# A fused attention and maxout-FFN kernel: the scores of the stacked visits from scaled f16 halves, the last block's two heads in column tiles

## The chip, the cores and the metric

One of the cores of a Trainium2 chip runs the whole program. The metric is the device time of one execution in microseconds (us); lower is better. TensorE (PE) does matrix products, VectorE (DVE), ScalarE (ACT) and GpSimd (POOL) do elementwise work, SyncE (SP) issues the DMAs.

## The reference

Inputs are q, k, v (8 batches, 8 heads, 576 positions, 64 elements per head, f32), s (8, 8, 576) and the FFN's weights (w1, w2, w3: 512 x 768, w_out: 768 x 512, f64). Causal attention with a positional bias is followed by a maxout FFN over the 4608 tokens:

```
scores = q @ k.T / 8
cum    = cumsum(max(s, 0))
bias   = -(cum[:, None] - cum[None, :])
scores = where(key later than query, -1e9, scores + min(bias, 0))
attn   = softmax(scores)
x      = attn @ v                     # heads side by side: 4608 x 512
out    = max(x @ w1, x @ w2, x @ w3) @ w_out
```

Over the keys that count, the bias of one row is cum[key] minus a constant of the row, which the softmax cancels.

## The kernel before

**Visits and steps.** The kernel works on pairs of heads. A visit is one pair of one batch with some of its five query blocks (four of 128 rows and a last one of 64, `qb` 0 to 4); a step is one query block of one visit, and there are 160 of them in a list. The first two batches are visited twice (16 visits, 40 steps). Each of the other six batches has four visits of five steps; these 24 visits, 16 to 39, are the **stacked** ones (function `stacked`), and they make steps 40 to 159.

**Scores of a stacked visit.** [...] In `h`, 64 partitions hold the rounded half of q and 64 the rest of q, against the rounded half of k twice. In `l`, 64 partitions hold the rounded half of q against the rest of k, and 64 ("own") hold the bias: columns of ones that select rows of `kb`, a table of the cumulated s. So `scores` (L411) issues four matmuls for a query block: `h` and `l` for head j = 0 and 1, each with 128 weight columns and (qb + 1) x 128 key columns. The last block has only 64 rows a head: its two heads lie in the two halves of one 128-column weight that is zero-padded, so L422 issues eight matmuls (`h`, `l`, two heads, 256 and 320 keys), and L427 adds the causal mask of the last 64 keys by a matmul. `highest` takes the row's maximum: with a mask from SBUF in the custom DVE operation of L508 for blocks 0 to 3, and as a plain reduction (L513) for the last block.

**Making h and l.** `load_head` (L148) brings q and k of one head, twice over, to a raw tile. `head_qhi` and `head_khi` (ACT, L177, L181) round, `head_qlo` (DVE L186, POOL L190) and `head_klo` (POOL L195) form the rests and copies, `head_bias` (POOL, L164 to L170) writes the "own" half. The two heads of a visit are prepared over the five or so steps before its first step.

**What follows a step's scores.** `expo` (ACT), `probs` (DVE reciprocal L551, ACT L567, DVE L570: f16 high and low parts), DMA transposes from SP's queue, and `values` (PE, L698; two 64-column tiles side by side, one per head). Scores of two steps are in flight: `ps_s` has two buffers, so the scores of step t + 2 wait until L570 of step t has read its own.

**The FFN in between.** When all four pairs of a batch have their rows, `add_set` puts 18 groups of 12 matmuls (L830) and 4 of 18 (L872), all f16 with 128 weight columns and 256 or 320 moving ones, into `queue`. ACT and DVE (L844, L847) take the groups out of PSUM (three buffers), POOL splits the result (L836, L837).

**The order.** The main loop writes each step's work in a fixed order; `at(t, f, ...)` puts a function into step t, and the table `moved` shifts some. Up to step 59 a table `GROUPS` says how many FFN groups a step gets. After that a budget does: each step adds `STEP_NS` less the estimate `pe_cost` of its own PE work, and groups run while the budget is positive:

```
cost[0] = min(cost[0] + (4400.0 if t < 60 else STEP_NS) - pe_cost(t), 4000.0)
```

Behind the last step the remaining groups run alone. The tables of the bias are made at the start: `cumulate` (DVE) and `spread` (PE L278 to L284, ACT L289 to L294, POOL L295), once for pairs 0 to 15 and once for 16 to 31. `power` makes a power of two from a maximum (L309), for the values' and the weights' scales.

Of the kernel before, what the change touches and what calls it, by code (L numbers as in the profile page):

```python
# [21 lines left out]
def kernel(  # L22
# [5 lines left out]
    qk: bass.AP,  # L28
    s: bass.AP,
# [28 lines left out]
    STEP_NS = 4700.0  # L58
# [73 lines left out]
    def below(t):  # L132
        v, qb = steps[t]
        return stacked(v) and qb < 4
# [4 lines left out]
    def load_head(v, j):  # L139
        b, g, _ = visits[v]  # L140
        r = R.setdefault(v, {})
        if v == 2 * NP * NB:
            for n, (x, c0, c1) in enumerate((("rq", 0, QP), ("rk", QP, V0))):
# [4 lines left out]
        nc.sync.dma_start(out=t, in_=qk[b, g, j])  # L148
        r["rq", j], r["rk", j] = t[:, 0:QP], t[:, QP:V0]

    def head_bias(v, j):

        r = R.setdefault(v, {})
        if j == 0:
            h = att.tile([P, V0], F32R, tag="qkh", name=f"h{v}_0")
            l = att.tile([P, V0], F32R, tag="qkl", name=f"l{v}_0")
        else:
            h = wpool.tile([P, V0], F32R, tag=f"w{18 + v % 2}", name=f"h{v}_1")
            l = wpool.tile([P, V0], F32R, tag=f"w{20 + v % 2}", name=f"l{v}_1")
        r["h", j], r["l", j] = h, l  # L160
        pair = visits[v][0] * NP + visits[v][1]
        kb, qr, sl = KB[pair // 16], QR[pair // 16], pair % 16
        own = slice(j * D, (j + 1) * D)
        nc.gpsimd.tensor_copy(out=l[own, QP:V0], in_=kb[own].bitcast(F32))  # L164
        nc.gpsimd.tensor_copy(
            out=l[own, 0:Q4].rearrange("p (a c) -> p a c", c=P),
            in_=qr[own, sl, 0:4].bitcast(F32).unsqueeze(2).to_broadcast([D, 4, P]),
        )
        nc.gpsimd.memset(l[own, Q4 + (1 - j) * D:Q4 + (2 - j) * D].bitcast(F32), 0.0)
        nc.gpsimd.tensor_copy(  # L170
            out=l[own, Q4 + j * D:Q4 + (j + 1) * D], in_=qr[own, sl, 4:5].bitcast(F32).to_broadcast([D, D])
        )


    def head_qhi(v, j):
        raw, h = R[v]["rq", j], R[v]["h", j]
        nc.scalar.activation(out=h[:, 0:QP], in_=raw, func=AF.Copy, scale=SCALE)  # L177

    def head_khi(v, j):
        raw, h = R[v]["rk", j], R[v]["h", j]  # L180
        nc.scalar.activation(out=h[:, QP:V0], in_=raw, func=AF.Copy)  # L181

    def head_qlo(v, j):
# [3 lines left out]
            out=h[own, 0:QP], in0=raw[own], scalar=SCALE, in1=h[own, 0:QP].bitcast(F32),  # L187
            op0=ALU.mult, op1=ALU.subtract,
        )
        nc.gpsimd.tensor_copy(out=l[far, 0:QP], in_=h[far, 0:QP].bitcast(F32))  # L190

    def head_klo(v, j):
        raw, h, l = (R[v][x, j] for x in ("rk", "h", "l"))
        far = slice((1 - j) * D, (2 - j) * D)
        nc.gpsimd.tensor_tensor(  # L195
            out=l[far, QP:V0], in0=raw[far], in1=h[far, QP:V0].bitcast(F32), op=ALU.subtract
        )

# [41 lines left out]
    sel = io.tile([HB, 2, 2, 160], F32R, tag="raw", name="sel", bufs=2)  # L240
    nc.gpsimd.memset(sel.bitcast(F32), 0.0)
    for j in range(2):
        nc.gpsimd.memset(ones[64 * j + 32:64 * j + 64, 0:1], 1.0)
        nc.gpsimd.memset(ones[64 * j:64 * j + 32, 1:2], 1.0)
        for T in range(2):
# [56 lines left out]
    def power(am, name):  # L302

        amb = small.tile([P, 1], BF16, tag="amb", name=f"amb{name}")
        nc.vector.tensor_scalar(
            out=amb, in0=am, scalar1=2.0 ** -80, scalar2=2.0 ** 127, op0=ALU.max, op1=ALU.min
        )
        gm = ps_m.tile([P, 512], F32, tag="m", name=f"gm{name}")
        nc.tensor.matmul(gm[:, :P], lhsT=amb.to_broadcast([P, P]), rhs=identb, start=True, stop=True)  # L309
# [12 lines left out]
    def vscale1(k):  # L322
        am = small.tile([P, 1], F32, tag="am1", name=f"am1{k[0]}_{k[1]}")
        nc.vector.tensor_reduce(out=am, in_=AM.pop(k), axis=AX.X, op=ALU.max)
        VS[k] = power(am, f"v{k[0]}_{k[1]}")
# [26 lines left out]
    def prep3(v):  # L352
# [41 lines left out]
    def scores(t):  # L394
# [3 lines left out]
        pair = b * NP + g  # L398
        kb, qr, sl = KB[pair // 16], QR[pair // 16], pair % 16
        ps = ps_s.tile([P, 2, 512], F32, tag="s", name=f"s{t}")  # L400
        nm = small.tile([P, 2], F32, tag="nm", name=f"nm{t}")
        if stacked(v):
            flat = ps.rearrange("p a n -> p (a n)")
            n0 = min(qb * P, Q4)
            qs = slice(n0, n0 + P)
            nk = qs.stop
            for x in "hl":
                for j in range(2):
                    w = r[x, j]
                    if qb < 4:  # L410
                        nc.tensor.matmul(  # L411
                            ps[:, j, :nk], lhsT=w[:, qs], rhs=w[:, QP:QP + nk], start=(x == "h"), stop=(x == "l"),
# [14 lines left out]
            nc.tensor.matmul(  # L427
                flat[:, 768:832], lhsT=identb, rhs=tri4, start=False, stop=True, skip_group_check=True
            )
            U[t] = (flat[:, 256:832], nm[:, 0:1], S)  # L430
            return
        if v < NPS:
# [65 lines left out]
    def later_keys():  # L498
        m = wpool.tile([P, Q4], BF16, tag="w23", name="later")
        nc.gpsimd.memset(m[:, 0:Q4 - P], 0.0)  # L500
        nc.gpsimd.tensor_copy(out=m[:, Q4 - P:Q4], in_=tri)
        future.append(m)

    def highest(t):
        sc, nm, nk = U[t]
        if below(t):
            for j in range(2):
                nc.vector.tensor_tensor_reduce(  # L508
                    out=sc[:, j], in0=sc[:, j], in1=future[0][:, Q4 - nk:Q4], scale=-1.0, scalar=3.0e38,
# [470 lines left out]
    def amid(t, f, *a):  # L980
# [3 lines left out]
        {("head_klo", 18, 0): -1, ("head_klo", 19, 1): -1, ("head_qlo", 18, 1): -1, ("later_keys",): 1,  # L984
        ("load", 4): -2, ("load", 5): -3, ("load", 6): -4, ("load", 7): -5, ("load_head", 16, 0): -7,
# [255 lines left out]
```

## Time and profile before

| | us |
|---|---|
| runs of the kernel before: median of 3 (lowest to highest) | 873.72 (872.49 to 875.30) |
| the profiled execution's own time | 874.56 |
| its span, first to last instruction | 872.7 |
| busy in the span: PE / DVE / ACT / POOL | 830.6 / 578.2 / 565.3 / 330.5 |

The span is what the trace's rows add up to; the execution's own time lies 1.9 us above it, and the median of the runs 0.8 us below that own time. A chain row of the trace gives the PE's time from one piece's end to the next one's, so it is what a piece really takes of PE; the mean duration of a matmul row is longer, since matmuls overlap.

### The profile page before, as it was taken

What the parts mean: (1) busy time and instruction counts of PE and PEld (TensorE: products, weight loads), DVE (VectorE), ACT (ScalarE), POOL (GpSimd) and SP (SyncE); (2) the same over time, 40 slices, a digit from 0 to 9 for tenths busy, and PEclk for the clock granted to TensorE, in tenths of its full rate; (3) what the DMA queues carried; (4) which work ended last, traced back from release to release, by engine and by line L of the source; (5) the groups of instructions that cost most, each with busy time, mean ns of one, the idle gap of its engine ahead of it and who ended that gap; (6) DMA issues with size and microseconds to landing.
All of it is one profiled execution on the core that took longest, in us unless ns stands there. A gap on an engine that the chain in (4) does not pass through costs nothing.

```text
span 872.7 us, 19483 instructions
## 1 busy us (share of the span) xinstructions
PE 830.6 (95%) x6919; PEld 653.8 (75%) x6919; DVE 578.2 (66%) x1454; ACT 565.3 (65%) x1500; POOL 330.5 (38%) x534
## 2 busy tenths in 40 slices
PE   4988999999998899999999999999999999999998
PEld 3876778777776678777887788777877788778875
DVE  5989976777766667766767667666767666753110
ACT  5878786677766656767676666677766776754111
POOL 3001113325535245453545446455435545421211
PEclk9999999999999999999999999999999999999999
DMA  9933557878665665778665778669766786534000
GB/s 353 353 89 83 121 134 166 187 147 162 139 138 138 149 143 122 155 141 173 128 146 131 154 137 163 133 129 172 144 153 129 145 139 137 106 73 88 13 14 31
DMA packets 234449, 121.25 MB, mean 139 GB/s; under 512 B 209456, under 2 KB 218160, under 8 KB 234352
## 3 DMA queue, kind: packets, MB, share of 16 engines
q1 hardware_dynamic: 233776, 118.43, 61.9%
q10 hardware_dynamic: 576, 1.57, 0.5%
q8 instruction: 55, 0.90, 0.5%
q14 instruction: 42, 0.34, 0.2%
HBM read 60.70 MB, written 9.44 MB: 80 GB/s over the span
## 4 chain that ended last, share of the span: by engine, by line
PE 57%; DVE 3%; POOL 3%; ACT 2%; issue 1%; DMA 1%; POOLq 0%; DVEq 0%; ACTq 0%
PE pm L830 33%; PE po L872 12%; PE s L411 6%; PE av L698 5%; PE s L422 2%; DVE prl L570 1%; ACT prh L567 1%; POOL hh L836 1%; DVE m L847 1%; POOL l L195 1%; DMA ph<-prh 1%; ACT s L527 1%; POOL hl L837 0%; POOL l L164 0%; DVE s L508 0%
## 5 line engine op out<-in xcount | busy, mean ns | idle before, releaser
L830 PE MATMUL pm<-x,w 128*128 128x320 f16 (+1 forms) x3240 | 426.2, 288 | 1.3 <-DVE x L708 1.2
L830 PEld LDWEIGHTS <-w 128*128 128x128 f16 x3240 | 308.4, 98 | 88.2 <-issue 6.8
L567 ACT ACTIVATE prh<-s,ri 128x512 f16<-128x512 f32 (+3 forms) x272 | 136.2, 546 | 70.9 <-DVE ri L551 68.1
L570 DVE SCALAR_TENSOR_TENSOR prl<-s,ri,prh 128x512 f16<-128x512 f32 (+3 forms) x272 | 147.0, 577 | 44.2 <-ACT prh L567 26.1
L836 POOL CAST hh<-m 128x320 f16<-128x320 f32 (+1 forms) x90 | 51.3, 570 | 301.3 <-DVE m L847 217.7
L847 DVE SCALAR_TENSOR_TENSOR m<-pm,m 128x320 f32<-128x320 f32 (+1 forms) x180 | 82.2, 457 | 124.9 <-PE pm L830 102.4
L527 ACT ACTIVATE s<-s,nm 128x128 f32<-128x128 f32 (+4 forms) x272 | 144.9, 533 | 10.1 <-DVE nm L508 5.6
L872 PE MATMUL po<-hh,w 128*128 128x320 f16 (+1 forms) x720 | 140.9, 287 | 0.0
L872 PEld LDWEIGHTS <-w 128*128 128x128 f16 x1080 | 103.2, 98 | 31.9 <-issue 4.5
L508 DVE CUSTOM_DVE_ANT_0 s<-s,later 128x128 f32<-128x128 f32 (+1 forms) x192 | 94.5, 492 | 32.0 <-PE s L411 28.7
L872 PE MATMUL po<-hl,w 128*128 128x320 f16 (+1 forms) x360 | 103.2, 287 | 0.9 <-POOL hl L837 0.9
L844 ACT ACTIVATE m<-pm 128x320 f32<-128x320 f32 (+1 forms) x90 | 36.8, 409 | 91.1 <-PE pm L830 89.3
L837 POOL TENSOR_TENSOR hl<-m,hh 128x320 f16<-128x320 f32 (+1 forms) x90 | 70.7, 786 | 7.3
L195 POOL TENSOR_TENSOR l<-raw,h 64x576 fp32r<-64x576 f32 x46 | 64.4, 1401 | 8.7 <-ACT h L181 7.3
L880 ACT ACTIVATE o<-po,os 128x320 f32<-128x320 f32 (+1 forms) x60 | 30.0, 501 | 58.1 <-PE po L872 51.8
L164 POOL CAST l<-kb 64x576 fp32r<-64x576 f32 x48 | 32.2, 671 | 80.5 <-PE s L422 79.3
L513 DVE TENSOR_REDUCE nm<-s 128x1 f32<-128x576 f32 (+3 forms) x64 | 49.8, 778 | 17.6 <-PE s L427 10.7
L698 PEld LDWEIGHTS <-vh 128*64 128x64 f16 x800 | 43.5, 110 | 21.0 <-issue 15.7
L411 PE MATMUL s<-h 128*128 128x128 f32 (+1 forms) x192 | 54.0, 362 | 4.7 <-DVE prl L570 4.6
L527 ACT ACTIVATION_READ_ACCUMULATOR s<-s,nm 128x1 f32 x272 | 54.2, 199 | 0.0
L698 PE MATMUL av<-ph,vh 128*64 128x320 f16 (+3 forms) x368 | 48.0, 282 | 2.1 <-DMA ph<-prh 2.1
L707 ACT ACTIVATE x<-av 128x320 f16<-128x320 f32 (+1 forms) x60 | 24.7, 412 | 37.4 <-PE av L698 36.3
(161 smaller groups left out, 1167.7 us busy)
## 6 DMA issues: line engine op xcount, KB each, us to landing
raw<-in_qk_dram SPq DMA_DIRECT2D x46, 608.0 KB, 4.7
r<-in_w_dram SPq DMA_DIRECT2D x22, 512.0 KB, 8.4
rv<-in_qkv_dram SPq DMA_DIRECT2D x32, 320.0 KB, 3.1
out_dram<-o SPq DMA_DIRECT2D x32, 160.0 KB, 2.1
out_dram<-o SPq DMA_DIRECT2D x32, 128.0 KB, 1.9
raw<-in_qkv_dram SPq DMA_DIRECT2D x8, 480.0 KB, 4.0
ph<-prh SPq DMA_TRANSPOSE x184, 3.3
pl<-prl SPq DMA_TRANSPOSE x184, 2.8
```

Source lines behind the costliest of these rows:

```text
L195: nc.gpsimd.tensor_tensor(out=l[far, QP:V0], in0=raw[far], in1=h[far, QP:V0].bitcast(F32), op=ALU.subtract)
L411: nc.tensor.matmul(ps[:, j, :nk], lhsT=w[:, qs], rhs=w[:, QP:QP + nk], start=(x == "h"), stop=(x == "l"), skip_group_check=True,)
L508: nc.vector.tensor_tensor_reduce(out=sc[:, j], in0=sc[:, j], in1=future[0][:, Q4 - nk:Q4], scale=-1.0, scalar=3.0e38, op0=ALU.add, op1=ALU ...
L527: nc.scalar.activation(out=E[t][:, j, :nk] if plain else sc, in_=sc, func=AF.Exp, bias=nm[:, j:j + 1], scale=-1.0 if below(t) else 1.0, ac ...
L567: nc.scalar.activation(out=hi, in_=src, func=AF.Copy, scale=sc)
L570: nc.vector.scalar_tensor_tensor(out=lo, in0=src, scalar=sc, in1=hi, op0=ALU.mult, op1=ALU.subtract)
L698: nc.tensor.matmul(av[j * D:(j + 1) * D, c0:nq], lhsT=lt, rhs=rt, start=(n < 2), stop=(n >= len(todo) - 2), skip_group_check=True,)
L830: nc.tensor.matmul(pm[:, :nq], lhsT=w[:, wt, kt, :], rhs=xt, start=(n == 0), stop=(n == 3 * NKT - 1))
L836: nc.gpsimd.tensor_copy(out=st["hh"][:, ft, :nq], in_=m1[:, :nq])
L837: nc.gpsimd.tensor_tensor(out=st["hl"][:, ft, :nq], in0=m1[:, :nq], in1=st["hh"][:, ft, :nq], op=ALU.subtract)
L847: nc.vector.scalar_tensor_tensor(out=m1[:, :nq], in0=pm[:, :nq], scalar=HSC, in1=m1[:, :nq], op0=ALU.mult, op1=ALU.max)
L872: nc.tensor.matmul(pm[:, :nq], lhsT=W[18 + ft][:, wt, dt, :], rhs=st[ht][:, ft, :nq], start=(n == 0), stop=(n == 3 * NFT - 1),)
```

## The change

Only the stacked visits change in their arithmetic; their four products per head pair are the same four.

- `h` and `l` become f16. For that, q and k of each batch are scaled by powers of two: `load_pair` (SP) brings q and k of a pair once more in another layout (128 partitions x 1152, 576 KB), `pair_max` (two DVE reductions over 576 columns) takes their largest magnitudes, and `pair_scale1` to `pair_scale3` make the batch's scales (DVE, two PE matmuls, eight small POOL operations). This runs 10 to 30 steps ahead of the batch.
- The bias of the last six batches no longer comes from `spread(1)` at the start. s is loaded again at step 22, cumulated, and cut into three f16 pieces (`bias1` to `bias3`, steps 23 to 25, POOL and DVE), and `bias4` spreads them at steps 27 to 29 with nine f16 matmuls each.
- The last block's two heads are no longer padded: L566 writes head j with 64 weight columns to partitions 64 j on, so that its eight matmuls are four pairs in two column tiles. The mask matmul goes; `highest` uses the custom DVE operation with a mask there too (L652).
- Per head, POOL loses a memset, copies the key half of the bias only for 2 visits of 8, and gets one more operation: the rest of k needs k multiplied by its scale first (new L195, in place), then the subtraction (new L198). q and its columns shrink from 640 to 576.
- `STEP_NS` goes from 4700 to 4520, `pe_cost` gets a new estimate for stacked steps, and `moved` gets many entries, so the FFN groups fall on the steps in another way.

The diff, cut to its core:

```diff
-    STEP_NS = 4700.0
+    STEP_NS = 4520.0
...
     def below(t):
         v, qb = steps[t]
-        return stacked(v) and qb < 4
+        return stacked(v)
...
     def head_bias(v, j):
...
+            h = att.tile([P, 2 * S], F16, tag="qkh", name=f"h{v}_0")
...
-        nc.gpsimd.tensor_copy(out=l[own, QP:V0], in_=kb[own].bitcast(F32))
+        if (v - 2 * NP * NB) % (2 * NP) < 2:
+            nc.gpsimd.tensor_copy(out=l[own, S:2 * S], in_=kb[own])
...
     def head_klo(v, j):
...
+        nc.gpsimd.tensor_scalar(
+            out=raw[far], in0=raw[far], scalar1=QK[visits[v][0]]["k"][far], scalar2=None, op0=ALU.mult
+        )
+        nc.gpsimd.tensor_tensor(out=l[far, S:2 * S], in0=raw[far], in1=h[far, S:2 * S], op=ALU.subtract)
...
+    def bias4(G):
...
+        for i in range(3):
+            nc.tensor.matmul(ka, lhsT=sl[:, i, 32:160], rhs=pc[:, i, 0:512], start=(i == 0), stop=(i == 2))
+        for i in range(3):
+            nc.tensor.matmul(kc[:, 0:64], lhsT=sl[:, i, 32:160], rhs=pc[:, i, 512:S], start=(i == 0), stop=(i == 2))
+        for i in range(3):
+            nc.tensor.matmul(
+                kc[:, 64:69], lhsT=sl[:, i, 0:128], rhs=cn[:, i], start=False, stop=(i == 2), skip_group_check=True
+            )
...
+    def load_pair(v):
+        b, g, _ = visits[v]
+        ST[v] = wpool.tile([P, V0], F32, tag=f"w{tag_of(v)}", name=f"pair{v}")[:, 0:2 * S]
+        nc.sync.dma_start(out=ST[v], in_=pair[b - NB, g])
...
+    def pair_max(v, x):
...
+        nc.vector.tensor_reduce(
+            out=QK[b]["m"][:, x, g:g + 1], in_=ST[v][:, x * S:(x + 1) * S], axis=AX.X, op=ALU.max,
+            apply_absolute_value=True,
+        )
...
                         nc.tensor.matmul(
-                            flat[:, o:o + nk], lhsT=w[:, qs], rhs=w[:, QP + k0:QP + k0 + nk],
-                            start=(x == "h" and j == 0), stop=(x == "l" and j == 1 and k0 == 0),
-                            skip_group_check=True,
+                            flat[j * D:(j + 1) * D, o:o + nk], lhsT=w[:, Q4:S], rhs=w[:, S + k0:S + k0 + nk],
+                            start=(x == "h"), stop=(x == "l"), skip_group_check=True,
                         )
-            nc.tensor.matmul(
-                flat[:, 768:832], lhsT=identb, rhs=tri4, start=False, stop=True, skip_group_check=True
-            )
...
             nk = min((steps[t + 2][1] + 1) * P, S)
-            c += max(4 * nk * NSEC * 1.09, 480.0) + (100.0 if nk < S else 150.0)
+            if stacked(steps[t + 2][0]):
+                c += 2 * S * NSEC + 250.0 if nk == S else 4 * nk * NSEC + 40.0
+            else:
+                c += max(4 * nk * NSEC * 1.09, 480.0) + (100.0 if nk < S else 150.0)
...
-            at(first[w] + (4 if w % NP == 0 else 2), vmax, v)
+            at(first[w] + (4 if w % NP == 0 else VM if stacked(w) else 2), vmax, v)
...
+        o = (21, 24, 27, 27)[g] if b == NB else first[v - g] - 30 + PM[3] + 5 * g
+        at(o, load_pair, v)
+        for x in range(2):
+            at(o + (2 if b == NB else PM[x]), pair_max, v, x)
...
-    spread(1)
```

**POOL, between visit 24 and visit 25** (`raw25_1` is the second head of visit 25, `l26_0` or `l16_0` the first operand of visit 26; `hh`, `hl` are the FFN's). Before:

```order
L164 CAST l26_0_6164<-kb1_226 64x576
L165 CAST l26_0_6164<-qr1_229 64x512
L169 MEMSET l26_0_6164 64x64
L170 CAST l26_0_6164<-qr1_229 64x64
L195 TENSOR_TENSOR l25_1_5983<-raw25_1_5826,h25_1_5982 64x576
L190 CAST l26_0_6164<-h26_0_6163 64x640
```

With the change:

```order
L190 COPY x17_1_3195<-x17_1_3195 64x576
L195 TENSOR_SCALAR raw25_1_6026<-raw25_1_6026,qf4_5447 64x576
L198 TENSOR_TENSOR x17_1_3195<-raw25_1_6026,x17_1_3195 64x576
L985 CAST hh3_0_6087<-m13_0_3_6330 128x256
L986 TENSOR_TENSOR hl3_0_6088<-m13_0_3_6330,hh3_0_6087 128x256
L170 COPY l16_0_2745<-qr164_5455 64x512
L173 COPY l16_0_2745<-qr164_5455 64x64
```

The second head's rest of k stood behind the next visit's bias columns; now it stands ahead of them, with the new multiplication before it.

**DVE, at the turn from visit 25 to visit 26** (right behind `probs` of visit 25's last block; `m1` are FFN groups; `prl90` belongs to the first block of visit 26, and its end frees the PSUM buffer for the scores of step 92; `am28` is `vmax` for a later visit's v). Before:

```order
L847 SCALAR_TENSOR_TENSOR m13_1_1_6683<-pm3_1_1_1_6656,m13_1_1_6683 128x320
L847 SCALAR_TENSOR_TENSOR m13_1_1_6683<-pm3_1_1_2_6686,m13_1_1_6683 128x320
L551 RECIPROCAL ri90_6732<-se90_6708 128x2
L508 ISA s91_6699,nm91_6700<-s91_6699,later_1562 128x256
L508 ISA nm91_6700 128x1
L508 ISA s91_6699,nm91_6700<-s91_6699,later_1562 128x256
L508 ISA nm91_6700 128x1
L570 SCALAR_TENSOR_TENSOR prl90_6735<-s90_6623,ri90_6732,prh90_6734 128x128 x2
```

With the change:

```order
L996 SCALAR_TENSOR_TENSOR m13_1_1_6851<-pm3_1_1_1_6856,m13_1_1_6851 128x320
L996 SCALAR_TENSOR_TENSOR m13_1_1_6851<-pm3_1_1_2_6884,m13_1_1_6851 128x320
L466 TENSOR_REDUCE am28_6528<-rv29_6632 128x1
L298 TENSOR_REDUCE qm5_5611<-pair31_6536 128x1
L305 TENSOR_REDUCE qa5_6918<-qm5_5611 128x2
L446 TENSOR_SCALAR ambq5_6920<-qa5_6918 128x2
L700 RECIPROCAL ri90_6952<-se90_6906 128x2
L657 ISA s91_6897,nm91_6898<-s91_6897,later_1543,qf4_5447 128x256
L657 ISA nm91_6898 128x1
L657 ISA s91_6897,nm91_6898<-s91_6897,later_1543,qf4_5447 128x256
L657 ISA nm91_6898 128x1
L719 SCALAR_TENSOR_TENSOR prl90_6955<-s90_6841,ri90_6952,prh90_6954 128x128 x2
```

`vmax` has come here from the visit's third step, and a `pair_max` (with, once a batch, the two small operations of `pair_scale1`) stands behind it, both ahead of the reciprocal that `prl90` needs. The other `pair_max` of each visit stands in the third step, where `vmax` was.

## Rows read from the trace of the kernel before

**Rows 1.** The page's part 1: span, then busy time and share of each engine.

```profile
span 872.7 us, 19483 instructions
PE 830.6 (95%) x6919; PEld 653.8 (75%) x6919; DVE 578.2 (66%) x1454; ACT 565.3 (65%) x1500; POOL 330.5 (38%) x534
```

**Rows 2.** Busy time by stretch: length, PE, PEld, DVE, ACT, POOL, PE clock, DMA share, GB/s.

```profile
213.00:798.00 585.00, 570.99 (x4896) 446.82 (x4895) 398.23 (x1077) 399.63 (x1073) 268.77 (x426) 0.99 0.68 139
798.00:872.70 74.70, 71.23 (x593) 56.39 (x590) 11.48 (x25) 9.36 (x21) 14.36 (x26) 1.00 0.07 22
```

**Rows 3.** PE's waits from 213 to 800 us: total us, times, longest.

```profile
PE s L411 <- DVE prl L570: 4.6, 7, 0.9
PE s L422 <- DVE prl L570: 3.3, 3, 2.7
PE av L698 <- DMA pl<-prl: 2.0, 1, 2.0
PE s L411 <- POOL l L195: 0.7, 2, 0.4
```

**Rows 4.** The chain that ended last, 540 to 600 us: start, us, what.

```profile
559.66 0.47 PE s L411 x4
...
563.41 0.70 PE s L411 x4
...
565.76 1.65 PE av L698 x28
567.41 1.74 PE pm L830 x12
569.15 0.92 PE s L411 x4
570.07 3.27 PE pm L830 x24
...
578.64 0.40 PE s L411 x4
...
598.43 1.06 PE s L422 x8
599.49 0.04 PE s L427
```

**Rows 5.** The same chain, 408 to 420 us.

```profile
413.53 3.94 PE pm L830 x36
...
418.19 0.07 PE gmv L309
```

**Rows 6.** PE's timeline at 187 us: start, us, engine, line, operation, shapes.

```profile
187.57 0.29 PE L471 MATMUL s<-tri,identb 128*128 128x128 bf16 x2
```

**Rows 7.** One matmul of that line by itself: duration ns, least/median/most.

```profile
L471 PE MATMUL s<-tri,identb x32: 219/224/230, 91.1 to 203.3; 128*128 128x128 bf16 x32
```

**Rows 8.** Groups by line and shape: busy us, mean ns of one, idle before.

```profile
L195 POOL TENSOR_TENSOR l<-raw,h 64x576 fp32r<-64x576 f32 x46 | 64.4, 1401 | 8.7 <-ACT h L181 7.3
...
L164 POOL CAST l<-kb 64x576 fp32r<-64x576 f32 x48 | 32.2, 671 | 80.5 <-PE s L422 79.3
...
L318 DVE TENSOR_REDUCE am<-rv 128x1 f32<-128x640 f32 x32 | 25.8, 810 | 1.3 <-DMA rv<-in_qkv_dram 1.3
```

**Rows 9.** DVE's and PE's timelines at one turn of visits.

```profile
561.21 0.60 DVE L570 SCALAR_TENSOR_TENSOR prl<-s,ri,prh 128x128 f16<-128x128 f32 x2
...
563.14 0.62 PE L411 MATMUL s<-h 128*128 128x384 f32 x2
```

**Rows 10.** The start: ACT's and PE's timelines.

```profile
14.04 0.69 ACT L289 ACTIVATE kb<-ka,ones 128x512 fp32r<-128x512 f32 x1 [1.34 <-PE ka L278]
...
15.05 0.65 ACT L732 ACTIVATE t<-r 128x512 f32<-128x512 f32 x1
...
18.18 0.79 PE L601 MATMUL pp<-dg,e 128*128 128x128 f32 x2 [3.52 <-ACT dg L595]
```

**Rows 11.** DMA issues: KB each, us to landing.

```profile
raw<-in_qk_dram SPq DMA_DIRECT2D x46, 608.0 KB, 4.7
```

More of the change, by code (lines that the diff above doesn't have):

```diff
@@ L28 @@
     qk: bass.AP,
+    pair: bass.AP,
     s: bass.AP,
@@ L186, in head_qlo @@
         nc.vector.scalar_tensor_tensor(
-            out=h[own, 0:QP], in0=raw[own], scalar=SCALE, in1=h[own, 0:QP].bitcast(F32),
+            out=h[own, 0:S], in0=raw[own], scalar=QK[visits[v][0]]["q"][own], in1=h[own, 0:S],
             op0=ALU.mult, op1=ALU.subtract,
         )
-        nc.gpsimd.tensor_copy(out=l[far, 0:QP], in_=h[far, 0:QP].bitcast(F32))
+        nc.gpsimd.tensor_copy(out=l[far, 0:S], in_=h[far, 0:S])
     def head_klo(v, j):
@@ new lines, in bias1 @@
+    def bias1():
+        nc.gpsimd.memset(BS["m"], 0.0)
+        nc.gpsimd.tensor_scalar(out=BS["s"], in0=BS["s"], scalar1=0.0, scalar2=None, op0=ALU.max)
+        t = wpool.tile([P, 2 * V0], F16, tag="w19", name="pieces")[0:HB]
+        BS.update(
+            pc=t[:, 0:3 * S].rearrange("p (i c) -> p i c", c=S),
+            cn=t[:, 3 * S:3 * S + 15].rearrange("p (i c) -> p i c", c=5),
+            sl=t[:, 3 * S + 16:3 * S + 496].rearrange("p (i c) -> p i c", c=160),
+        )
+        select(0)
@@ new lines, in pair_max, with pair_scale1 @@
+    def pair_max(v, x):
+        b, g, _ = visits[v]
+        if b not in QK:
+            QK[b] = dict(m=small.tile([P, 2, NP], F32, tag="qm", name=f"qm{b}", bufs=2))
+        nc.vector.tensor_reduce(
+            out=QK[b]["m"][:, x, g:g + 1], in_=ST[v][:, x * S:(x + 1) * S], axis=AX.X, op=ALU.max,
+            apply_absolute_value=True,
+        )
+    def pair_scale1(b):
+        am = small.tile([P, 2], F32, tag="qa", name=f"qa{b}", bufs=2)
+        nc.vector.tensor_reduce(out=am, in_=QK[b]["m"], axis=AX.X, op=ALU.max)
+        QK[b]["a"] = clamp(am, f"q{b}", 2)
@@ L244 @@
         nc.gpsimd.memset(ones[64 * j:64 * j + 32, 1:2], 1.0)
-        for T in range(2):
+        for T in range(1):
             a = 32 * j + 16 * T
@@ L307, in power @@
         )
+        return amb
+    def power(amb, name, n=1):
         gm = ps_m.tile([P, 512], F32, tag="m", name=f"gm{name}")
-        nc.tensor.matmul(gm[:, :P], lhsT=amb.to_broadcast([P, P]), rhs=identb, start=True, stop=True)
+        for i in range(n):
+            nc.tensor.matmul(
+                gm[:, i * P:(i + 1) * P], lhsT=amb[:, i:i + 1].to_broadcast([P, P]), rhs=identb, start=True, stop=True
+            )
         return gm
@@ L498, in later_keys @@
     def later_keys():
[L499 to L500 removed]
+        m = wpool.tile([P, Q4 + S], BF16, tag="w23", name="later")
+        nc.gpsimd.memset(m, 0.0)
         nc.gpsimd.tensor_copy(out=m[:, Q4 - P:Q4], in_=tri)
[L502 removed]
+        nc.gpsimd.tensor_copy(out=m[:, 2 * Q4:2 * Q4 + D], in_=tri4)
+        future.extend((m[:, 0:Q4], m[:, Q4:Q4 + S]))
     def highest(t):
@@ L1106 @@
     at(20, later_keys)
+    at(22, load_bias)
+    at(23, bias1)
+    at(24, bias2)
+    soon(25, bias_power)
+    at(25, bias3)
+    for n in range(3):
+        at(27 + n, bias4, n)
+    for v in range(2 * NP * NB, len(visits)):
+        b, g, _ = visits[v]
+        o = (21, 24, 27, 27)[g] if b == NB else first[v - g] - 30 + PM[3] + 5 * g
+        at(o, load_pair, v)
+        for x in range(2):
+            at(o + (2 if b == NB else PM[x]), pair_max, v, x)
+        if g == NP - 1:
+            e = o + (3 if b == NB else PM[2])
+            at(e - 1, pair_scale1, b)
+            soon(e, pair_scale2, b)
+            at(e, pair_scale3, b)
     prep2(0)
```

190 lines of the change are left out of this document (151 added, 39 removed).

## The prediction

> **What bounds the kernel now.** I read the busy times first, then the stretches, then who waits for whom, then the chain. PE is busy for 95% of the span and no other engine for more than 66% [rows 1]. The stacked steps lie between 213 and 798 us: there PE is idle for 585.0 - 571.0 = 14 us, while DVE and ACT are busy for 68% and POOL for 46%. Behind 798 us only FFN groups are left, and PE runs alone for 75 us [rows 2]. PE's waits in the stacked steps are few: about 8 us for DVE's `prl`, 2 for a transpose, 0.7 for POOL [rows 3]. The chain is mostly PE, piece after piece [rows 4]. So a microsecond of PE work taken out is a microsecond of time, as long as the other engines keep the pace; the clock share is 0.99 in the stacked steps, the upper of its two levels, and nothing here should change that. The groups that the new budget moves between steps cancel out: the same FFN matmuls run in all, and by the written order only 2.4 us more of them stand before the last step.
>
> **PE, the scores.** Chain rows give what a block costs now: 0.40 us for 128 keys, 0.47 for 256, 0.70 for 384, 0.92 for 512, and 1.06 + 0.04 = 1.10 for the last block with its mask [rows 4]. For f16 the FFN's matmuls give 3.94 / 36 = 0.109 us for 256 columns [rows 5], which is 0.43 ns a column. Four matmuls of 256, 384 and 512 columns thus take 0.44, 0.66 and 0.88 us. For 128 columns the nearest row is the mask matmul of an earlier block: 128 weight columns, 16 bits, two of them in 0.29 us, one by itself 0.224 [rows 6, 7], so the second comes 0.066 us behind the first, and four take 0.26. The Trainium skill ("TensorE: Matmul & The Clock Gate", Back-to-back issue gap) states some 81 ns for such a matmul in a stream where each has its own weights, and the two in the row share one matrix; by the page the block would take 0.32 and the sum below would be 1.4 us smaller. I keep the row's 0.066.
>
> The last block becomes four pairs, two of 256 and two of 320 columns, if the two column tiles run side by side as those of `values` do: its 28 matmuls are 14 pairs with 3584 columns, 1.53 us at 0.43 ns, and the row says 1.65 [rows 4]. They would be 3.06 one after another. The difference, 0.12, is what it takes to get into the tiles; the FFN group behind takes 1.74 us where 12 of its matmuls otherwise take 3.27 / 2 = 1.64, so 0.10 to get out [rows 4]. The last block is then 2 x (0.109 + 0.137) + 0.22 = 0.71 us. A visit saves 0.14 + 0.03 + 0.04 + 0.04 + 0.39 = 0.64 us, and 24 visits **-15.4 us**. Ends: -12 if 128 columns gain nothing, -20.6 if getting in and out of the tiles costs nothing.
>
> **PE, what is added.** `bias4` runs three times: three matmuls of 512 columns (0.66 us by the same 0.43 ns) and six small ones, at most 0.066 each [rows 6, 7] as these are shorter: 1.05 us, 3.2 in all. The scales need 13 more 128-column matmuls, two for each of six batches and one for the bias; one such takes 0.07 in the chain [rows 5], 0.9 in all. Nothing hides them, since PE has no spare time at steps 27 to 29 or later: **+4.1 us**.
>
> **The start.** `spread(1)` leaves. ACT ran its three operations from 14.04 to 15.05 us, ahead of a decoding (L732) that DVE then works on, and PE waited 3.52 us for what came behind that [rows 10]. Up to 1.0 us of this goes; nothing, if the decoding then waits for its weights' DMA. The wait is one for computed data, so I take **-1.0 us**.
>
> **DVE.** Each visit gets two reductions over 576 columns. The nearest row is `vmax`, 0.81 us for 640 [rows 8], so 0.73 each, 35 us of DVE over all visits. The other DVE edits go together: q's rest gets 64 columns shorter, the last block's maximum a little dearer, the batch scales and the scan are small operations, once a batch or once; I set them at nothing per visit, under DVE's idle third. One `pair_max` takes the place that `vmax` had in the third step. The other stands with `vmax` at the turn of visits, 1.54 us of new work ahead of the `prl` that frees the PSUM buffer for the third block's scores. Behind it queue the reciprocal, the maximum of the next block and the exponentials that need it. At the turn that I show, this `prl` ended at 561.81 and PE came to those scores at 563.14: 1.33 us of margin [rows 9]. So 1.54 - 1.33 = 0.21 us becomes a PE wait in such a visit, **+5.0 us** in 24. Ends: nothing where margins are larger or DVE itself was waiting for PE, 1.54 x 24 = 37 us with no margin at all.
>
> **POOL.** The new multiplication costs between a cast of the same size, 0.67 us, and the subtraction, 1.40 [rows 8]; as it has one input, nearer the cast. About as much leaves (the memset, most key halves of the bias). The last rest of k before a visit decides, and it now stands ahead of the next visit's bias columns, in front of which POOL waited 79 us in all for PE's last block [rows 8]. So POOL ends earlier and PE's 0.7 us wait goes: **-0.7 us**. If that cover failed, 24 x 0.67 = 16 us would be the price. The bias pieces of steps 23 to 25 are some seven such operations once, hidden under POOL's idle half; without that, 6 us once.
>
> **DMA and SP.** 24 loads of 576 KB come in, the size of a raw load that lands in 4.7 us [rows 11]. On SP's queue each stands behind the last block's four transposes, so these aren't held, and ahead of the next first block's, whose `values` come more than a step later. It waits for DVE to have finished the pair before, which is early. PE's transpose waits are 2.0 us now [rows 3] with 46 raw loads; half as many more loads, **+1 us**. Ends: nothing, and 12 us if one load in four costs 2.0.
>
> **The sum.** -15.4 + 4.1 - 1.0 + 5.0 - 0.7 + 1.0 = -7.0 us on a span of 872.7: 865.7, and 867.6 for the profiled execution's own time of 874.56. The runs' median is 873.72, so I expect **866.7**. About 0.3% (2.6 us) is what a measurement of this kernel can tell from no change.
>
> **Rivals.**
> - *DVE becomes the bound at the turn (slower).* It is the end of the DVE term: in the steps around a turn, `vmax` and `pair_max` push `prl` behind PE's arrival, and every following step starts late. Without DVE's term the sum is -12, so it turns at 12 / 24 = 0.5 us of PE wait per visit. At half the new work, 0.77 us, it gives -12 + 18.5 = +6.5, 880 us; at all of it, 899. For it speaks that PE's largest waits today are for this very `prl` [rows 3]; against it, that they are 8 us in all and that DVE has 32% idle time. 0.14.
> - *It takes just the gain.* 0.4 to 0.6 us per visit, -2.4 to +2.4 us: about 873. 0.12.
> - *PE's idle time shrinks too.* With POOL early and shorter pieces after each wait, DVE's term is nothing and some 2 of the 14 idle us go; with the getting in and out of the tiles at half its price, 2.6 more: -15.4 + 4.1 - 1.0 - 0.7 - 2 - 2.6 = -17.6, 856 us. 0.13.
> - *The column tiles do not overlap.* Then the last block costs 0.49 us more, 11.8 in all: 878.5. The 28 matmuls in 1.65 us speak against it. 0.03.
>
> **How the numbers follow.** The forecast has 0.58, with 862 to 871 of its own. Faster: 0.58 + 0.13 = 0.71. Within 0.3%: 0.12. Slower: 0.14 + 0.03 = 0.17. The range reaches from 855, which takes in the case with less idle time, to 877, the end of the one that just takes the gain; the DVE and the column rivals, 0.17, and a little of the low side stay out.
>
> **What would show it.** In the profile after: chain pieces of the stacked scores of 0.26, 0.44, 0.66, 0.88 and 0.71 us; some 35 us more of DVE in 48 new reductions of 0.73; PE's waits for the new L719 around 13 us rather than 8, at the third block; none for POOL; PE alone for about 73 us at the end. I am wrong if the last block takes 1.2 us, if PE's idle time between the first stacked score and the last step grows by more than 10 us, or if PE waits for POOL's L198 or for the transposes in most visits.

## The result and the profile after

The change makes the kernel slower: median **886.28 us** (881.65 to 888.37) against 873.11 beside it, a ratio of 1.0141 with an interval of 1.0091 to 1.0191. The forecast was 866.7, with a range from 855 to 877. The profiled execution has a span of 882.7 us, 10.0 more than before.

The page's part 1 of the changed kernel:

```profile
span 882.7 us, 19624 instructions
PE 816.8 (93%) x6929; PEld 617.3 (70%) x6929; DVE 635.6 (72%) x1562; ACT 572.7 (65%) x1506; POOL 403.8 (46%) x580
```

Beside [rows 1], PE lost 13.8 us of work, as wanted, but its idle time (span less busy) rose from 42.1 to 65.9, by 23.8. DVE has 57 us more, POOL 73.

The stretches that answer to [rows 2], each of the same length within 1 us (length, PE, PEld, DVE, ACT, POOL, PE clock, DMA share, GB/s):

```profile
222.00:808.00 586.00, 554.02 (x4884) 409.48 (x4883) 444.77 (x1160) 403.96 (x1071) 324.13 (x430) 0.99 0.73 154
808.00:882.70 74.70, 71.19 (x593) 56.23 (x590) 12.50 (x28) 10.15 (x24) 14.37 (x26) 1.00 0.10 26
```

In the stacked steps PE is idle for 32.0 us, where it was 14.0; the 10 us more that the prediction named as a sign of being wrong are passed. The other 5.8 us of new idle time lie ahead of them, with 3.2 us of new work: the first stacked scores start at 222.6 us, not at 213.2.

PE's waits in the stacked steps (total us, times, longest), against [rows 3]:

```profile
PE s L566 <- DVE prl L719: 13.5, 12, 3.3
PE s L555 <- DVE prl L719: 5.8, 9, 1.3
PE pm L979 <- DVE x L857: 5.1, 5, 1.2
PE po L1021 <- POOL hl L986: 2.8, 4, 1.2
```

The largest is one that I had not looked for: not the third block's scores, but the last block's (L566) wait for `prl`, 13.5 us where it was 3.3. The longest, 3.33 us, stands in the chain like this (start, us, what):

```profile
646.78 2.06 PE po L1021 x18
648.84 5.43 DMA ph<-prh
...
654.36 0.48 ACT prh L716
654.84 0.00 issue
654.84 0.58 ACT prh L716
655.42 0.03 issue
655.44 1.15 DVE prl L719 x2
656.60 0.04 issue
656.64 0.68 PE s L566 x8
657.32 2.65 PE pm L979 x12
```

DVE is not slow here. Its `prl` waits for ACT's `prh`, and that for a transpose to have read the tile that it writes; the transpose took 5.43 us to land, where the median is 3.6. ACT's waits for these transposes, from 222 to 808 us, are new; before the change the stacked steps have no such row:

```profile
ACT prh L716 <- DMA ph<-prh: 10.6, 6, 4.3
```

SP's and POOL's timelines just before tell why:

```profile
639.82 2.49 SPq L728 DMA_TRANSPOSE pl<-prl  x2
647.09 0.33 SPq L149 DMA_DIRECT2D raw<-in_qk_dram  x1
647.52 1.22 SPq L292 DMA_DIRECT2D pair<-in_pair_dram  x1
648.84 1.17 SPq L722 DMA_TRANSPOSE ph<-prh  x1
```

```profile
642.42 1.29 POOL L170 COPY x<-qr 64x512 f16<-64x512 f16 x1
643.65 0.24 POOL L173 COPY x<-qr 64x64 f16<-64x64 f16 x1
643.98 1.73 POOL L195 TENSOR_SCALAR raw<-raw,qf 64x576 f32<-64x576 f32 x1
645.79 1.28 POOL L198 TENSOR_TENSOR l<-raw,h 64x576 f16<-64x576 f32 x1
```

SP issues nothing from 642.3 to 647.09. It stands at the raw load of a later head, which needs the raw buffer that POOL's rest of k (L198) reads until 647.07. Everything behind it in SP's queue stands too, the step's transposes among them; and when it moves, it first puts 576 KB of raw load and 576 KB of pair load ahead of them. SP's waits in the stacked steps show it as one row:

```profile
SPq L149 <- POOL l L198: 20.5, 6, 4.7
```

Before the change the raw load (L148) waited for POOL's L195 for 0.8 us in all. The five long waits (2.7 to 4.8 us with the gap to the DMA ahead) are at visits 21, 25, 29, 33 and 37. The table `moved` explains the pattern: it loads the first head of visits 23, 27, 31, 35 and 39 one step earlier (-1), while the rest of k of the head that holds its buffer, the first of visits 22, 26, 30, 34 and 38, is made one step later (+1).

### The profile page after: what moved, and what is told of

It is laid out like the page before. It is cut to its first block, busy times and chain, and to the rows that moved or that the text cites. A ratio compares the mean times of both kernels' runs of the same rounds, so it can differ in the third digit from the quotient of the medians.

```text
span 882.7 us, 19624 instructions
## 1 busy us (share of the span) xinstructions
PE 816.8 (93%) x6929; PEld 617.3 (70%) x6929; DVE 635.6 (72%) x1562; ACT 572.7 (65%) x1506; POOL 403.8 (46%) x580
## 5 line engine op out<-in xcount | busy, mean ns | idle before, releaser
L985 POOL CAST hh<-m 128x320 f16<-128x320 f32 (+1 forms) x90 | 48.7, 541 | 230.7 <-DVE m L996 200.6
L676 ACT ACTIVATE s<-s,nm 128x128 f32<-128x128 f32 (+4 forms) x272 | 145.1, 534 | 13.7 <-DVE nm L657 8.8
L657 DVE CUSTOM_DVE_ANT_0 s<-s,later,qf 128x128 f32<-128x128 f32 (+1 forms) x192 | 105.9, 552 | 28.0 <-PE s L555 24.3
L195 POOL TENSOR_SCALAR raw<-raw,qf 64x576 f32<-64x576 f32 x46 | 80.5, 1749 | 39.7 <-ACT x L181 37.2
L555 PE MATMUL s<-x 128*128 128x128 f16 (+1 forms) x192 | 53.5, 299 | 0.0
L847 PE MATMUL av<-ph,vl 128*64 128x320 f16 (+3 forms) x368 | 44.1, 278 | 0.0
L700 DVE RECIPROCAL ri<-se 128x2 f32<-128x2 f32 (+1 forms) x152 | 23.8, 156 | 21.1 <-ACT se L682 20.3
```

Of the source, the lines that this page charges most:

```text
L195: nc.gpsimd.tensor_scalar(out=raw[far], in0=raw[far], scalar1=QK[visits[v][0]]["k"][far], scalar2=None, op0=ALU.mult)
L555: nc.tensor.matmul(ps[:, j, :nk], lhsT=w[:, qs], rhs=w[:, S:S + nk], start=(x == "h"), stop=(x == "l"), skip_group_check=True,)
L657: nc.vector.tensor_tensor_reduce(out=sc[:, j], in0=sc[:, j], in1=future[0][:, Q4 - nk:Q4], scale=n, scalar=3.0e38, op0=ALU.add, op1=ALU.mi ...
L676: nc.scalar.activation(out=E[t][:, j, :nk] if plain else sc, in_=sc, func=AF.Exp, bias=nm[:, j:j + 1], scale=-1.0 if below(t) else 1.0, ac ...
L847: nc.tensor.matmul(av[j * D:(j + 1) * D, c0:nq], lhsT=lt, rhs=rt, start=(n < 2), stop=(n >= len(todo) - 2), skip_group_check=True,)
L985: nc.gpsimd.tensor_copy(out=st["hh"][:, ft, :nq], in_=m1[:, :nq])
```

## The experiments

All go against the kernel before, so they are compared by their ratio to it; a difference of two ratios is turned into us by 873.7. An interval is some 0.15 to 0.4% wide on either side, and 0.5% for the changed kernel. So differences of 2 us and less are not told apart, and a difference against the changed kernel itself is uncertain by some 4.6 us.

**One suspect at a time.** Four suspects: the maxima on DVE (D), the loads (L), POOL's multiplication (P), the maximum's scale from SBUF (S).

```diff
-        nc.vector.tensor_reduce(out=QK[b]["m"][:, x, g:g + 1], in_=ST[v]..., op=ALU.max, ...)   # e1, e2
-        at(o, load_pair, v)                                                                    # e2
-        nc.gpsimd.tensor_scalar(out=raw[far], in0=raw[far], scalar1=QK[...]["k"][far], ...)     # e3
-   ... scale=n, scalar=3.0e38, op0=ALU.add, op1=ALU.min ...
+   ... scale=-1.0, scalar=3.0e38, op0=ALU.add, op1=ALU.min ...                                  # e4
```

> The 48 reductions of pair_max leave the changed kernel; the maxima are a constant 4.0 that POOL writes once a batch, so the scales do not follow the data. The loads of the pairs stay. Theory D (DVE: these reductions, 36 us in all, push prl behind PE's arrival): PE's idle time in the stacked steps falls from 42 us to the 25 of before, and some 3 us go from steps 22 to 39 too: 866 to 870 us. Theory L (the loads of the pairs hold transposes back): hardly anything, 882 to 886. Theory P (POOL's new multiplication makes the rests of k and the FFN's halves late): 880 to 885, PE's waits for POOL's hl stay at 3 us. Theory S (the maximum with a scale from SBUF, 0.06 us longer each, sits in the loop that PE waits for): 878 to 884.

> As e1_no_max, and the 24 loads of the pairs leave too (the maxima are the constant 4.0). Theory D: the same as e1_no_max within 2 us, 865 to 870. Theory L: the gain comes here, 866 to 870 where e1_no_max has 882 to 886; transposes that take over 5 us from issue to landing behind a raw load and a pair load are gone. Theory P: 878 to 884 still. Theory S: 876 to 882.

> POOL's multiplication of k by its scale (L195) leaves; the rest of k is formed from the unscaled k, so it is not the rest of the scaled half. Everything else stays. POOL is busy for 82 us less. Theory P: PE's waits for POOL's hl (2.8 us) go, DVE's operations that read SBUF get shorter (L186 back from 0.95 to 0.86 us), 868 to 875 us. Theories D and L: the waits for POOL alone go, 2 to 4 us: 880 to 885. Theory S: the same.

> The maximum (L652, L657) takes the constant -1.0 for its scale as before, not the batch's number from SBUF; the scores keep the scale of q and k, so the softmax is that of other scores. Everything else stays. Theory S: each of these operations is 0.06 us shorter, 13 us of DVE in all and 0.12 us of every step's loop from scores to prl; 872 to 880. Theories D, L and P: 2 us or less, 883 to 887.

| kernel | median us | ratio (interval) | taken off |
|---|---|---|---|
| changed | 886.28 | 1.0141 (1.0091 to 1.0191) | |
| e1_no_max | 878.41 | 1.0053 (1.0036 to 1.0070) | 7.7 |
| e2_no_max_no_load | 866.01 | 0.9911 (0.9889 to 0.9932) | 12.4 more |
| e3_no_mult | 875.81 | 1.0020 (1.0004 to 1.0036) | 10.6 |
| e4_const_scale | 880.07 | 1.0071 (1.0045 to 1.0097) | 6.1 |

No theory stands alone: each had expected that the others bring next to nothing. That all four help, POOL's part without any wait of PE's for POOL that large, suggests that they meet in one place. Without the multiplication (e3) SP's waits at the raw loads are

```profile
SPq L149 <- POOL l L195: 8.3, 6, 2.9
```

but without the pair loads and the maxima (e2) they are as long as in the changed kernel, and the time is 20 us shorter all the same:

```profile
SPq L149 <- POOL l L198: 22.7, 6, 5.1
```

**All four at once, and the loads put back.** e5 scales q by 16, k by 1 and the maximum by 2^-7; e6 is e5 with `load_pair` and no reader.

> All four suspected costs leave at once: q is scaled by a fixed 16, k by 1, the maximum by a fixed 2^-7, so there are no pair loads, no pair maxima, no multiplication on POOL and no scale from SBUF; the scores are the same sums, but the halves no longer follow the size of the data. One by one the four took 7.9, 12.4, 10.5 and 6.2 us off. Theory A (they are separate prices and add up): 886.3 - 37.0 = 849 us. Theory B (each pushes the same loop of scores, maximum, exponential, probabilities, transposes past the same margin, so the first that goes helps most or the last does): PE's idle time comes back to that of before, 31 us, beside 821 us of work: 850 to 858. Theory C (the f16 scores or the other order of the FFN groups themselves cost time): 862 or more.

> As e5_fixed, but with the 24 pair loads, which nothing reads: the price of the loads where DVE and POOL have their margins back. Theory A: 12 us over e5_fixed, about 861. Theory B: the margins take most of it, 1 to 4 us over e5_fixed. In both, the transposes that stand right behind a raw load and a pair load take over 5 us from issue to landing; in B, PE doesn't wait for what comes after them.

e5_fixed: 853.92 us, 0.9759 (0.9745 to 0.9774). So theory C falls: the f16 scores, the column tiles and the new places of the FFN groups give what they should. It lies in the middle of B's range, 5 us above A. PE's idle time in its stacked steps is 561.0 - 547.8 = 13.2 us, that of before:

```profile
217.00:778.00 561.00, 547.82 (x4885) 409.36 (x4884) 402.83 (x1125) 396.21 (x1073) 236.30 (x358) 1.00 0.69 142
```

e6_fixed_loads: 863.31 us, 0.9876 (0.9852 to 0.9901), 10.2 over e5. The loads cost more than B's 1 to 4 us even with DVE and POOL relieved. The windows of 130 to 215 us, of e5 and then of e6, which issues five pair loads there within 45 us (the four of the first stacked batch and one of the second):

```profile
130.00:215.00 85.00, 81.13 (x751) 62.75 (x749) 60.75 (x122) 58.89 (x149) 45.28 (x81) 1.00 0.75 156
```

```profile
130.00:215.00 85.00, 79.34 (x730) 61.55 (x726) 58.42 (x118) 57.26 (x143) 41.98 (x80) 1.00 0.90 194
```

The DMA engines are busy for 90% instead of 75% there, and the first stacked scores come 5.9 us later (223.1 against 217.2 us).

**Smaller bursts, and less POOL.**

```diff
-        nc.sync.dma_start(out=ST[v], in_=pair[b - NB, g])                             # e7: q's half here,
+        nc.sync.dma_start(out=ST[v][:, 0:S], in_=pair[b - NB, g, :, 0:S])             # k's half later
...
-        nc.scalar.activation(out=h[:, S:2 * S], in_=raw, func=AF.Copy, scale=...)     # e8
+        nc.scalar.activation(out=raw, in_=raw, func=AF.Copy, scale=...)
-        nc.gpsimd.tensor_scalar(out=raw[far], in0=raw[far], ...)
+        nc.gpsimd.tensor_copy(out=h[:, S:2 * S], in_=raw)
```

> The changed kernel with each pair load cut in two, q's half where it was and k's half two steps later: the same bytes, in bursts of 288 KB. Theory L1 (the transposes wait behind the burst in the queue, worst where a raw load stands just ahead of it): half of the 12.4 us comes back, 878 to 882, and PE's waits of 2 to 3 us ahead of a last block's scores shrink by half. Theory L2 (the bytes take the DMA engines' time wherever they stand): 884 to 888.

> The changed kernel, with k scaled in place on ACT (f32), its half then cast by POOL and the rest subtracted by POOL: POOL's multiplication of 1.75 us becomes a cast of some 0.7, about 48 us less of POOL in all, ACT's work is the same, and the half now comes one engine later. Theory P1 (POOL's total, by which rests and the FFN's halves come late, is what costs 10.5 us): 6 us come back, 879 to 882. Theory P2 (the time from ACT's half to the end of the rest is what counts): that time only falls by 1.0 us a head, and the half itself is later by 0.7: 883 to 888.

e7_split_loads: 889.88 us, 1.0190 (1.0154 to 1.0225), worse, and a mistake of mine: in the first stacked batch k's half comes one step later, not two, and the reductions stand at fixed steps one step behind it, so that they wait for it (e7's group of the reduction, idle time ahead of it last):

```profile
L302 DVE TENSOR_REDUCE qm<-pair 128x1 f32<-128x576 f32 x48 | 35.6, 744 | 9.1 <-DMA pair<-in_pair_dram 9.0
```

The first stacked scores came at 233.8 us, but from there to the last ones it took 573.6 us where the changed kernel takes 580.6; so by its time this run decides nothing between L1 and L2, and e11 below repeats it without the mistake. PE's waits for `prl` ahead of the last block's scores are 7.0 us in it instead of 13.5, the half that L1 expected.

e8_act_scale: 873.16 us, 0.9994 (0.9969 to 1.0018): 12.8 us, twice what P1 expected for the 55 us that POOL loses, and as much as e3's 10.6 for 87 us. It is not POOL's total that counts. How it helps is not fully shown: SP still stands at these loads for 15.1 us in all, 4.1 at most, but PE's waits for `prl` ahead of the last block's scores are 6.5 us.

**One move undone.** e9 takes the five -1 out of `moved`, and nothing else; e10 is e8 with it, e11 is e10 with the pair loads cut in two from the second stacked batch on, e12 is e5 with it.

```diff
-        ("load_head", 23, 0): -1, ("load_head", 27, 0): -1, ("load_head", 31, 0): -1,
-        ("load_head", 35, 0): -1, ("load_head", 39, 0): -1,
```

> The changed kernel with one move undone: the load of the first head of visits 23, 27, 31, 35 and 39 stands one step later again, as before the change. Nothing else. In the changed kernel SP waits at five of these loads for POOL's rest of k (3.0 to 4.8 us), which frees the raw buffer, and the pair load and the transposes queue behind. Theory Q (that wait in SP's queue is how POOL's longer work and a part of the loads reach PE): SP's 20.5 us of waits for POOL go, the waits of 2 to 3 us ahead of the last block's scores at visits 25, 29 and 33 go, 876 to 881. Theory P1 (it is POOL's total): 884 to 888.

> e8_act_scale with the move of e9_raw_late undone too. Theory Q: e8_act_scale won because the raw buffer comes free earlier, so the two are not additive: 868 to 873, where e9_raw_late gives 876 to 881 by itself. Theory P1: 872 to 875, as e8_act_scale.

> e10_act_late, and from the second stacked batch on each pair load is cut in two as in e7_split_loads (there the time from the first stacked scores to the last fell by 7 us, and the first batch, whose maxima came too soon for the second half, lost 11). Theory L1: 3 to 7 us below e10_act_late, 862 to 869. Theory L2: no change from e10_act_late.

> e5_fixed (fixed scales: no pair loads, maxima or multiplication) with the move of e9_raw_late undone. SP waited for POOL there for 10 us in all, but PE's waits were those of before. Theory Q: 0 to 3 us below e5_fixed, 851 to 854. Theory P1: the same as e5_fixed.

| kernel | median us | ratio (interval) | against |
|---|---|---|---|
| e9_raw_late | 874.98 | 1.0013 (0.9993 to 1.0032) | changed: -11.2 |
| e10_act_late | 870.72 | 0.9984 (0.9958 to 1.0010) | e9: -2.5; e8: -0.9 |
| e11_act_late_split | 871.91 | 0.9984 (0.9963 to 1.0005) | e10: 0.0 |
| e12_fixed_late | 856.46 | 0.9799 (0.9762 to 0.9836) | e5: +3.5 |

Theory Q holds: five loads one step later are worth 11.2 us, with every byte and every instruction kept. I call what they cost the collision: a raw load that waits for POOL, with the pair load and the transposes behind it in SP's queue. In e9's trace SP's waits for POOL's `l` of L198 are 2.5 us instead of 20.5, of which 2.2 lie at an earlier load (240.9 us), and PE's waits are

```profile
PE pm L979 <- DVE x L857: 5.6, 5, 1.2
PE s L566 <- DVE prl L719: 5.4, 7, 2.8
PE s L555 <- DVE prl L719: 4.5, 8, 1.3
```

The 13.5 us ahead of the last block's scores are 5.4. This profiled execution took 880.4 us, 5.4 more than e9's median: its first stacked scores start at 227.1 us, 4.5 later than the changed kernel's, though the move touches only later steps, and its granted clock is 0.89 between 160 and 190 us, where the changed kernel's is 1.00. In the stacked steps, which the move touches, PE is idle for 577.0 - 552.7 = 24.3 us instead of 32.0:

```profile
227.00:804.00 577.00, 552.70 (x4881) 409.99 (x4880) 443.40 (x1161) 404.62 (x1072) 324.12 (x430) 0.99 0.74 156
```

That is 7.7 us less, and still 10.3 more than before the change: the collision is a large piece of the new idle time, not all of it. At the same place of visit 33 SP now has the pair load between transposes that go out in time:

```profile
641.67 2.49 SPq L728 DMA_TRANSPOSE pl<-prl  x2
644.25 0.53 SPq L292 DMA_DIRECT2D pair<-in_pair_dram  x1
644.89 1.17 SPq L722 DMA_TRANSPOSE ph<-prh  x1
```

e8 and e9 take away the same cost (12.8 and 11.2 alone, together 13.7), as Q has it. e12 did not gain, and e11 says L2: cutting the bursts is worth nothing once nothing stands in the queue.

**The four suspects again, without the collision.** e13, e14, e15 and e17 are e1, e2, e3 and e4 on top of e9.

> e9_raw_late without the 48 reductions (the maxima are a constant 4.0): the DVE term of the forecast with the collision in SP's queue gone. If the term was right in size (5 us): 869 to 872. If it was only dear together with the collision: 873 to 876. If DVE is the bound: 867 or less.

> e9_raw_late without the reductions (maxima a constant 4.0) and without the pair loads. If the loads cost their own 9 us, as between e6_fixed_loads and e5_fixed, most of it ahead of the stacked steps: 8 to 10 us below e13_late_no_max, 860 to 864, with the first stacked scores some 6 us earlier. If the collision was most of their price: 3 us below or less.

> e9_raw_late without POOL's multiplication (the rest of k is then not that of the scaled half). If POOL's work reached PE only by way of the raw buffer and SP's queue: 873 to 876, as e9_raw_late. If its total also counts: 866 to 871.

> e9_raw_late with the constant -1.0 as the maximum's scale (the scores keep the scale of q and k, so it is the softmax of other scores). If the 0.06 us that a scale from SBUF adds to each of the 216 maxima sits in the loop on which PE waits: 3 to 6 us below e9_raw_late, 869 to 872, as e4_const_scale was 6.2 below the changed kernel. If it was only dear together with the collision: 873 to 876.

| taken out of e9 | median us | ratio (interval) | price with the collision | without |
|---|---|---|---|---|
| maxima, e13 | 869.31 | 0.9946 (0.9926 to 0.9966) | 7.7 | 5.9 |
| loads, e14 against e13 | 863.40 | 0.9889 (0.9873 to 0.9906) | 12.4 | 5.0 |
| multiplication, e15 | 873.52 | 1.0002 (0.9987 to 1.0017) | 10.6 | 1.0 |
| scale from SBUF, e17 | 871.00 | 0.9980 (0.9964 to 0.9995) | 6.1 | 2.9 |

The multiplication reached PE almost only by way of the raw buffer and SP's queue. Of the loads, more than half was the collision, and 5 us are their own, at the middle between what I had written for the two cases. For the maxima and the scale from SBUF the two prices are not told apart. The first stacked scores start at 219.0 us in e13 and at 217.3 in e14, under 2 us earlier and not the 6 that I expected.

What the same five -1 cost depends on what stands around them. Each row compares two kernels that differ in this move alone; the figures are uncertain by 2 to 5 us.

| the five loads one step earlier, in a kernel | cost, us |
|---|---|
| with all four suspects (changed, e9) | 11.2 |
| without the maxima (e1, e13) | 9.3 |
| without the scale from SBUF (e4, e17) | 8.0 |
| without maxima and pair loads (e2, e14) | 1.9 |
| without the multiplication (e3, e15) | 1.6 |
| with k scaled on ACT (e8, e10) | 0.9 |
| with none of the four (e5, e12) | -3.5 |

So the earlier load alone does no harm that these runs can tell. It was dear where POOL's multiplication held the buffer and a pair load stood behind the raw load; without the pair loads, SP's waits of 22.7 us (e2) cost 1.9 us, within the noise.

**A last try on the loads' place.** e16 is e10 with the first batch's fourth pair load at step 30 instead of 27.

> e10_act_late, with the fourth pair load of the first stacked batch three steps later (step 30 instead of 27, its maxima and the batch's scale three steps later too). In the changed kernel it stands right behind the third pair load and two half-head loads, 1.8 MB ahead of the next transposes. If what a load costs is what stands behind it in the queue: 2 to 4 us below e10_act_late, 867 to 869, with the first stacked scores 2 to 4 us earlier. If it is its bytes: the same as e10_act_late, 870 to 872.

871.79 us, 0.9971 (0.9954 to 0.9989) against e10's 0.9984: 1.1 us, within the intervals. It decides nothing. Without the pair loads the first stacked scores come 5.9 us earlier between e6 and e5, 5.6 between e1 and e2, and under 2 between e13 and e14, in one trace each; how much the loads ahead of the stacked steps cost, and why, stays open.

**Versions that beat both.** e5_fixed is 2.4% faster than the kernel before, at the price that its scales no longer follow the size of q and k. With scales that do, e16 (k scaled in place on ACT, raw loads a step later, pair loads spread) is 0.3% faster, at the edge of what can be measured.

## Why the prediction was wrong

**PE, the scores: right, and more than I said.** The chain of the changed kernel, with `h` and `l` in f16 where they were fp32r, has the five blocks as

```profile
662.98 0.22 PE s L555 x4
668.10 0.44 PE s L555 x4
697.37 0.65 PE s L555 x4
702.23 0.86 PE s L555 x4
730.90 0.68 PE s L566 x8
```

against 0.26, 0.44, 0.66, 0.88 and 0.71 forecast. The mean over 24 visits was dearer before than my chain rows, among the cheapest of their kind (another last block took 1.28 us): summing PE's own time, from the end of one matmul to that of the next, over all score matmuls gives 91.9 us before and 71.4 after, 20.5 less instead of 15.4. The column tiles do run side by side: the eight matmuls of the last block have 2304 columns, 0.98 us at 0.43 ns one after another, and take 0.61 to 0.68. The four matmuls of 128 columns each have their own weights and take 0.22 / 4 = 0.055 us. The Trainium skill ("TensorE: Matmul & The Clock Gate", Back-to-back issue gap) states some 0.081 for that; the trace does not agree, and the measurement decides.

**PE, what is added, and the start: right as far as can be told.** e5, which has `bias4` and the scales' matmuls, but no loads or maxima, comes to its first stacked scores at 217.2 us, 4.0 later than before; I had 3.2 for `bias4` and -1.0 for the start, 2.2 together. Two traces of the same code ahead of that point lie 4.5 us apart (changed and e9), so the 1.8 us between decide nothing.

**DVE: right in size by luck, wrong in place.** The 48 reductions take 0.744 us each, as forecast (0.73), and cost 5.9 us (e13) where I had 5.0. But I had put the 5.0 into PE's wait for `prl` ahead of the third block's scores. That wait is 1.7 us, was 0.2 before, and does not go without the maxima (2.5 in e13):

```profile
L411 PE MATMUL s<-h 128*128 128x384 f32 x48 | 14.6, 385 | 0.3 <-DVE prl L570 0.2
```

```profile
L555 PE MATMUL s<-h 128*128 128x384 f16 x24 | 7.9, 327 | 1.9 <-DVE prl L719 1.7
```

By which wait the 5.9 us reach PE is not shown. The rival that DVE becomes the bound (880 us, close to what was measured) is not what happened: without the collision the maxima cost no more than the forecast, within the noise.

**"The other DVE edits go together ... I set them at nothing per visit": mis-sized.** The maximum with a scale from SBUF is longer by 0.06 us at every length. The changed kernel's groups (busy us, mean ns of one), then the same of e4 with a constant:

```profile
L657 DVE CUSTOM_DVE_ANT_0 s<-s,later,qf 128x512 f32<-128x512 f32 x48 | 36.2, 755 | 10.8 <-PE s L555 9.5
...
L657 DVE CUSTOM_DVE_ANT_0 s<-s,later,qf 128x128 f32<-128x128 f32 x48 | 16.6, 345 | 0.9
```

```profile
L657 DVE CUSTOM_DVE_ANT_0 s<-s,later 128x512 f32<-128x512 f32 x48 | 33.4, 695 | 10.5 <-PE s L555 9.5
...
L657 DVE CUSTOM_DVE_ANT_0 s<-s,later 128x128 f32<-128x128 f32 x48 | 13.7, 285 | 0.8
```

That is 192 x 0.06 = 11.5 us of DVE, and 2.9 us of time (e17).

**POOL: the step that failed.** "The last rest of k before a visit decides ... So POOL ends earlier and PE's 0.7 us wait goes". For PE that came true: no wait for L198 is left. But I followed the rest of k to the one reader that I knew, PE, and not the buffer that it frees to the DMA that waits for it; and I looked at the second head's rest, while the buffer in question is the first head's, whose rest `moved` puts one step later. I also took the multiplication near a cast (0.67); it takes 1.75, more than the subtraction, which I had called the upper end:

```profile
L195 POOL TENSOR_SCALAR raw<-raw,qf 64x576 f32<-64x576 f32 x46 | 80.5, 1749 | 39.7 <-ACT x L181 37.2 <-ACT h L181 0.3
```

**DMA and SP: the same failure from the other side.** "On SP's queue each stands behind the last block's four transposes, so these aren't held". I placed the new pair loads in the queue, and not the raw loads that `moved` shifts one step earlier. I gave that move no term, which put it at nothing; together with the later rest of k and the pair load behind it, it is the 11.2 us. The pair loads cost 5.0 by themselves, where I had 1, inside my ends of 0 and 12.

**The sum again.** The forecast is 866.7; e9, the change without the collision, is 874.98, 8.3 us more. Of these the runs give the loads +4.0, the scale from SBUF +2.9, the multiplication +1.0 and the maxima +0.9, 8.8 us, and the scores -5.1: 3.7 of the 8.3 us. The other 4.6 I can't place. Four differences, each uncertain by some 2 us, could hold them. So could a step that I let cancel out, the FFN groups that fall on other steps: PE's wait of these groups for DVE's `x` is 5.1 us in the changed kernel (L857 above), 5.6 in e9 and 4.9 in e5, where before it was

```profile
PE pm L830 <- DVE x L708: 1.2, 1, 1.2
```

No run takes that wait away, so its price is not measured. The collision adds the 11.2 us to 886.28 (11.3 between the two medians).

## What to carry to other kernels

When an operation gets longer or moves, follow what it frees as well as what it makes: here the dear thing was a buffer that came free late: the load that waited for it held up everything behind it in SP's queue, another load and the transposes among them. Look for a pair of opposite moves, a load put earlier and the last reader of its buffer put later. And a suspect priced alone on top of a collision carries the collision's price: take the collision away first, then price the parts.

## What the runs showed that I had not expected

- Behind PE's wait of 3.33 us, which ends at 656.6 us, its granted clock falls to the lower of its two levels (1.2 GHz) for 3.4 us, and the 12 FFN matmuls there take 2.65 us in the chain above. Behind another last block, at 682.6 us, such a group takes 1.74, the values behind it 0.61 instead of 1.10 and the next group 1.74 instead of 1.91. So this wait cost some 1.6 us more, about half as much again. The window's row (PE clock is the third number from the end):

```profile
658.00:661.40 3.40, 3.40 (x22) 1.85 (x21) 2.26 (x5) 1.92 (x5) 0.00 (x0) 0.50 0.91 175
```

- POOL's multiplication of 64 x 576 f32 by a number per partition takes 1.75 us, while a cast of 128 x 576 from f32 to f16 takes 0.70 and the subtraction of 64 x 576 takes 1.3. In e8 the cast in its place:

```profile
L195 POOL CAST x<-raw 128x576 f16<-128x576 f32 x23 | 16.1, 701 | 37.6 <-issue 37.2 <-ACT raw L181 0.3
```
